# Linear attention and a squared-ReLU FFN on one core: attention chunks 4 to 9 in pairs on quarters of the array, chunks 10 to 23 by halves, the block-diagonal form dropped

## The chip, the core and the metric

The kernel runs on one core of one Trainium2 chip. The metric is the device time in microseconds of one execution; the median of the runs is compared.

## What is computed

The reference, cut to what matters (B = 4, H = 8, S = 768, D = 64, d_model 512, d_ff 2048):

```python
gamma = 1.0 - 2.0 ** (-5.0 - np.arange(H))
for t in range(S):
    state = gamma[None, :, None, None] * state + np.einsum('bhd,bhe->bhde', k[:, :, t], v[:, :, t])
    y[:, :, t] = scale * np.einsum('bhd,bhde->bhe', q[:, :, t], state)
x = y.transpose(0, 2, 1, 3).reshape(B * S, H * D)
h = np.maximum(x @ w_in, 0.0)
out = h * h @ w_out
```

So there is a decaying linear attention over 768 tokens in each of 4 sequences, and then a two-layer FFN on all 3072 tokens.

## The kernel before

The 3072 tokens are 24 chunks of 128 (6 to a sequence). Within a chunk the attention is done by matmuls: q and k are scaled by powers of gamma and cast to bf16, transposed, multiplied into scores, masked, and multiplied with v; a running state in PSUM (`c_ps`, copied to `s_bd`) carries what earlier chunks add. The FFN works on blocks of chunks, `BLOCKS = [4, 2, 2, ...]`: the first product fills `psf` tiles, ACT applies ReLU into `h`, DVE squares it in place, and the second product gives 128 output rows of 512, which ACT copies to `osb` and SP stores.

The schedule is written out by hand. Instructions go to each engine's queue in program order. The front (the calls after `keep_awake(8, ...)`) does chunks 0 to 3 and the first units of block 0, with `keep_awake` matmuls on an identity matrix in between. After that, the FFN is a stream of numbered pieces (`ffn_pieces`): block 0 has pieces 5 to 16 (first product) and 17 to 32 (second), block 1 has 33 to 40 and 41 to 48, block 2 has 49 to 56 and 57 to 64, and so on, 16 to a block. `put(n, step, ...)` hangs a step of the attention, a load or a cast behind piece n; `before(n)` issues these steps, and then the squares of that piece (`take_squares`), so a step on DVE stands in its queue behind the squares of the pieces before.

Three forms of attention are used:

- in pairs on quarters of the array (chunks 0 to 3, `PAIRED = 4`): two chunks at a time, matmuls of 64 rows by 64 columns in four positions of the array (`scores_pair`, `state_pair`, `outputs_pair`), and `finish_pair` with plain matmuls for what comes from the state;
- block-diagonal (chunks 4 to 11, `attend`): one chunk at a time, the two heads of a pair side by side with zeros off the diagonal (`k_bd`, `v_bd`, `s_bd`), in plain matmuls of 128 columns (`scores` L421, `state` L447, `outputs` L476 and L484). Chunks 4 to 7 are transposed on TensorE (L367, L380), chunks 8 to 11 by DMA and a copy on DVE (`spread_k`);
- by halves (chunks 12 to 23, `attend2`): half chunks of 64 tokens, plain matmuls with 64 columns (`scores2` L682, `state2` L709, `outputs2` L731 and L738), always with DMA transposes.

Blocks 1 and 2 run their first product one chunk at a time (`first_unit`, 128 columns); later blocks take both chunks at once (256 columns). `cast_w` and `cast_w_out` turn the fp32 weights into bf16 on POOL, DVE and ACT. `pack_constants` makes the constants of the half form.

Of the kernel before, what the change touches and what calls it, by code (L numbers as in the profile page):

```python
# [9 lines left out]
FP32 = mybir.dt.float32  # L10
# [9 lines left out]
LDBUFS = 4  # L20


PAIRED = 4

# [3 lines left out]
PACK_FROM = 12  # L28

GROUP = 3  # L30
# [3 lines left out]
def kernel(  # L34
# [32 lines left out]
    ldpool = ctx.enter_context(tc.tile_pool(name="ldpool", bufs=LDBUFS // 2))  # L67
    grpool = ctx.enter_context(tc.tile_pool(name="grpool", bufs=2))
    qspool = ctx.enter_context(tc.tile_pool(name="qspool", bufs=2))
    kspool = ctx.enter_context(tc.tile_pool(name="kspool", bufs=4))  # L70
# [34 lines left out]
    kv_tiles = {}  # L105

    def load_kv(m):
        b, i = chunks[m]
        for name, src, to in (("kn", k, raw_k), ("vn", v, raw_v)):
            if m % 2 == 0:  # L110
                kv_tiles[name] = ldpool.tile([P, 2 * H * D], FP32, name=name)
            t = kv_tiles[name].rearrange("s (c h d) -> s c h d", c=2, h=H)[:, m % 2]
            nc.sync.dma_start(t, src[b, :, i * C : (i + 1) * C, :].rearrange("h s d -> s h d"))
            to[m] = t

    def load(m):
        if m % 2 == 0:
            load_q(m)
        load_kv(m)

    def group_loads(m):

        b, i = chunks[m]
        for name, src, to in (("kg", k, raw_k), ("vg", v, raw_v)):
            t = grpool.tile([P, 2 * GROUP, NPAIR, D], FP32, name=name)
            for h in range(H):
                p, hh = divmod(h, 2)
                rows = slice(64 * hh, 64 * (hh + 1))
                nc.sync.dma_start(
                    t[rows, :, p, :],  # L130
                    src[b, h, i * C : (i + GROUP) * C, :].rearrange("(w s) d -> s w d", s=64),
                )
                yield
            for j in range(GROUP):
                to[m + j] = t[:, 2 * j : 2 * j + 2].rearrange("s u p d -> s (u p) d")
# [36 lines left out]
    def exponents(pattern, step, name, logs, parts=(slice(0, P),)):  # L172
# [15 lines left out]
    ex_k = exponents([[C, NCH], [0, H]], 1, "ex_k", lng)  # L188
    qf = const.tile([P, NCH, H], FP32)
    nc.scalar.activation(qf[:], ex_q[:], AF.Exp)  # L190
    kf = const.tile([P, NCH, H], FP32)
    kfp = const.tile([P, NCH, H], FP32)
    nc.scalar.activation(kfp[:], ex_q[:], AF.Exp, scale=-1.0)
    nc.scalar.activation(kf[:], ex_k[:], AF.Exp, scale=-1.0)
# [14 lines left out]
    cmask = const.tile([P, 2, C // 2], BF16)  # L209
    nc.gpsimd.memset(cmask[:], 0.0)  # L210
    nc.gpsimd.affine_select(
        out=cmask[:],
        in_=cmask[:],
        compare_op=ALU.is_gt,
        fill=1.0,
        base=0,
        pattern=[[-1, 2], [-2, C // 2]],
        channel_multiplier=1,
    )
# [39 lines left out]
    v_bds = [const.tile([P, NPAIR, 4, D], BF16, name=f"v_bd{j}") for j in range(4)]  # L259
    k_bds = [const.tile([P, NPAIR, 2, C], BF16, name=f"k_bd{j}") for j in range(2)]  # L260
    s_bds = [const.tile([P, NPAIR, 2, D], BF16, name=f"s_bd{j}") for j in range(3)]
    ks_bd2s = [const.tile([P, 2 * NPAIR, 2, D], BF16, name=f"ks_bdp{j}") for j in range(2)]

    v_bd2s = [t.rearrange("s p (c hh) d -> s (p c) hh d", hh=2) for t in v_bds[2:]]
    def zero_on_scalar(out, rows=slice(0, P)):
        shape = list(out.shape)
        nc.scalar.activation(
            out, ident[rows, None, 0 : shape[2]].to_broadcast(shape), AF.Copy, scale=0.0
        )

    for t in k_bds:
        nc.vector.memset(t[0:64, :, 1, :], 0.0)
        nc.vector.memset(t[64:128, :, 0, :], 0.0)
    for j, t in enumerate(v_bds[:2]):
        zero_on_scalar(t[:, :, 1:3, :].rearrange("s p hh d -> s p (hh d)"))
        if j < 2:
            zero_on_scalar(s_bds[j][0:64, :, 1, :], slice(0, 64))
            zero_on_scalar(s_bds[j][64:128, :, 0, :], slice(64, 128))
# [49 lines left out]
    def zero_off_diagonal(t, hh):  # L328
        nc.vector.memset(t[halves[hh], :, 1 - hh, :], 0.0)

# [11 lines left out]
    def scale_kv(m):  # L342
        b, i = chunks[m]
        ks = kspool.tile([P, H, D], BF16, name="ks")
        nc.vector.tensor_tensor(
            out=ks[:],
            in0=raw_k.pop(m)[:],
            in1=kf[:, i, :, None].to_broadcast([P, H, D]),
            op=ALU.mult,
        )  # L350
        v_bd = v_bds[m % 2]
        vn = raw_v.pop(m)
        nc.gpsimd.tensor_copy(  # L353
            v_bd[:, :, ::3, :], vn.rearrange("s (p hh) d -> s p hh d", hh=2)
        )
        at[m].update(ks=ks, v_bd=v_bd)

# [3 lines left out]

    def transpose_q(m, split=False):
        qs = at[m].pop("qs")
        tp = ps_tp.tile([P, 2, NPAIR, C], BF16, name="tp")
        for r in range(2):
            for p in range(NPAIR):
                nc.tensor.transpose(tp[:, r, p, :], qs[:, r, 2 * p : 2 * p + 2, :], ident[:])  # L367
        qT = qTpool.tile([P, 2, NPAIR, C], BF16, name="qT")
        if split:
            nc.scalar.activation(qT[:, 0], tp[:, 0], AF.Copy)  # L370
            nc.vector.tensor_copy(qT[:, 1], tp[:, 1])
        else:
            nc.scalar.activation(qT[:], tp[:], AF.Copy)
        give_qT(m, qT)

    def transpose_k(m, pool=ps_tp, name="tp", split=False):
        a = at[m]
        tp = pool.tile([P, 2, NPAIR, C], BF16, name=name)
        for p in range(NPAIR):
            nc.tensor.transpose(tp[:, 0, p, :], a["ks"][:, 2 * p : 2 * p + 2, :], ident[:])  # L380
        k_bd = k_bds[m % 2]
        for hh in range(2):
            rows = slice(64 * hh, 64 * (hh + 1))
            if split and hh == 1:
                nc.vector.tensor_copy(k_bd[rows, :, hh, :], tp[rows, 0, :, :])
            else:
                nc.scalar.activation(k_bd[rows, :, hh, :], tp[rows, 0, :, :], AF.Copy)
        a["k_bd"] = k_bd
# [9 lines left out]
    def dma_transpose_k(m):  # L398
        a = at[m]
        kT = kTpool.tile([P, 2 * NPAIR, C], BF16, name="kT")  # L400
        nc.sync.dma_start_transpose(kT[:, 0:NPAIR], a["ks"].rearrange("s h d -> s (h d)"))
        a["kT"] = kT

    def spread_k(m):
        a = at[m]
        kT = a.pop("kT")
        k_bd = k_bds[m % 2]
        for hh in range(2):
            rows = slice(64 * hh, 64 * (hh + 1))
            nc.vector.tensor_copy(k_bd[rows, :, hh, :], kT[rows, 0:NPAIR])  # L410
        a["k_bd"] = k_bd

    def scores(m, half, pool=ps_st, name="st"):
        a = at[m]
        if half == 0:
            a["pt"] = ptpool.tile([P, NPAIR, 2, C], BF16, name="pt")
        st = pool.tile([P, 2, 2, C], FP32, name=name)
        for pp in range(2):
            p = 2 * half + pp
            for hh in range(2):  # L420
                nc.tensor.matmul(  # L421
                    st[:, pp, hh, :],
                    lhsT=a["k_bd"][:, p, hh, :],
                    rhs=a["qT"][:, :, p, :],
# [623 lines left out]
```

## Time and profile before

| what | value |
|---|---|
| median of 3 runs | 215.16 us (215.15 to 215.17) |
| profiled execution | 214.9 us, of which the span from first to last instruction is 213.1 us |
| TensorE busy | 205.4 us (96%) |
| VectorE (DVE), ScalarE (ACT), GpSimd (POOL) busy | 130.2, 116.1 and 49.7 us |
| first FFN matmul | 19.0 us |
| last FFN matmul starts | 209.9 us |
| moved by DMA | 39.65 MB |

Times inside the profiled execution are counted from its first instruction. Busy time of TensorE adds up overlapped matmuls of a pipelined engine, so the mean duration of a matmul in a row is its latency, not the time that it holds the engine.

### The profile page before, as it was taken

To read this page: it belongs to the slowest core of one execution; us is meant where nothing else is said; L and a number is where in the kernel's file an instruction comes from. 1 tells how busy PE (TensorE), PEld (TensorE's weight loads), DVE (VectorE), ACT (ScalarE), POOL (GpSimd) and SP (SyncE) were. 2 spreads that over 40 slices of the span, in tenths; PEclk is the share of its full clock that TensorE was granted. 3 is DMA by queue.
4 is the path that set the end of the run, shared out by engine and by line. 5 is a ranking of instruction groups with operands and counts; after the bars stand their busy time and mean duration, and the time that the engine had idled before them with its cause. 6 is when DMAs were issued, how large, how long until landed. Compare 5 with 4: busy or idle time off the path is not lost.

```text
span 213.1 us, 5212 instructions
## 1 busy us (share of the span) xinstructions
PE 205.4 (96%) x2119; PEld 142.1 (67%) x2119; DVE 130.2 (61%) x257; ACT 116.1 (54%) x216; POOL 49.7 (23%) x106
## 2 busy tenths in 40 slices
PE   6888999999999999999999999999999999999994
PEld 1466644558966975875875875875965965965853
DVE  4796885165585696695495595593694693640410
ACT  8374885258853653652663663652753754643631
POOL 5332456321110411008122223033121223000000
PEclk9999999999999999999999999999999999999999
DMA  6999999999989796579999598799597432601102
GB/s 167 290 321 381 387 385 244 298 242 258 267 212 200 189 196 145 159 179 174 176 203 198 134 219 182 180 235 174 132 191 174 102 76 73 102 0 52 49 0 98
DMA packets 90551, 39.65 MB, mean 186 GB/s; under 512 B 66336, under 2 KB 84000, under 8 KB 90528
## 3 DMA queue, kind: packets, MB, share of 16 engines
q1 hardware_dynamic: 90528, 39.33, 78.8%
q8 instruction: 16, 0.26, 0.6%
q14 instruction: 7, 0.06, 0.1%
HBM read 27.26 MB, written 6.29 MB: 157 GB/s over the span
## 4 chain that ended last, share of the span: by engine, by line
PE 87%; DMA 5%; DVE 2%; POOL 2%; ACT 1%; issue 1%; SPq 1%; POOLq 0%; ACTq 0%
PE psf L778 38%; PE psf L836 37%; DMA qn<-in_q_dram 3%; DMA vn<-in_v_dram 2%; PE st L421 1%; PE y L484 1%; PE y L738 1%; PE st L682 1%; PE c_ps L709 1%; PE y L731 1%; POOL qs L507 1%; DVE pt L568 1%; DVE pt L428 1%; PE y L476 1%; PE c_ps L586 1%
## 5 line engine op out<-in xcount | busy, mean ns | idle before, releaser
L778 PE MATMUL psf<-xt,w_in_bf 128*128 128x256 bf16 (+2 forms) x880 | 90.6, 259 | 0.2 <-ACT xt L492 0.2
L836 PE MATMUL psf<-w_out_bf,h 128*128 128x512 bf16 (+2 forms) x400 | 89.6, 371 | 0.0
L778 PEld LDWEIGHTS <-w_in_bf 128*128 128x128 bf16 x880 | 71.4, 98 | 11.6 <-issue 0.3
L787 ACT ACTIVATE h<-psf 128x512 bf16<-128x512 f32 x96 | 56.9, 596 | 22.1 <-PE psf L778 19.4
L836 PEld LDWEIGHTS <-h 128*128 128x128 bf16 x400 | 36.3, 98 | 35.1
L758 DVE TENSOR_TENSOR h<-h 128x512 bf16<-128x512 bf16 x96 | 43.7, 472 | 20.6 <-ACT h L787 19.6
L846 ACT ACTIVATE osb<-psf 128x512 f32<-128x512 f32 (+2 forms) x25 | 14.5, 580 | 28.6 <-PE psf L836 28.5
L719 DVE CAST s_bd<-c_ps 64x256 bf16<-64x256 f32 x22 | 9.4, 428 | 27.0 <-ACT s_bd L718 26.8
L657 POOL CAST v<-vg 128x512 bf16<-128x512 f32 x12 | 7.7, 644 | 54.4 <-PE c_ps L709 19.5
L660 POOL CAST v_bd<-vg 64x512 bf16<-64x512 f32 x24 | 15.9, 664 | 17.6 <-PE y L738 16.9
L428 DVE TENSOR_TENSOR pt<-st,cmask 128x512 bf16<-128x512 f32 x16 | 11.1, 691 | 14.3 <-PE st L421 14.0
L644 DVE TENSOR_TENSOR ks_bdp<-kg,kf 64x512 bf16<-64x512 f32 x24 | 18.3, 763 | 0.4
L353 POOL CAST v_bd<-vn 128x512 bf16<-128x512 f32 x8 | 5.7, 718 | 36.5 <-PE y L484 22.6
L745 ACT ACTIVATE xt<-y 128x512 bf16<-128x512 f32 x12 | 8.9, 741 | 9.6 <-PE y L738 9.6
L334 DVE TENSOR_TENSOR qs<-qn,qf 128x1024 bf16<-128x1024 f32 x10 | 12.1, 1213 | 1.8 <-DMA qn<-in_q_dram 1.8
L718 ACT ACTIVATE s_bd<-c_ps 64x256 bf16<-64x256 f32 x22 | 8.1, 366 | 8.8 <-PE c_ps L709 8.8
L492 ACT ACTIVATE xt<-y 128x512 bf16<-128x512 f32 x8 | 6.0, 749 | 5.5 <-PE y L484 5.2
L301 POOL CAST w_out_bf<-w_stage 128x512 bf16<-128x512 f32 x12 | 7.5, 667 | 5.5 <-DMA w_stage<-in_moe_w_out_dram 5.5
L689 DVE TENSOR_TENSOR pt<-st,cmask 128x512 bf16<-128x512 f32 x12 | 8.3, 691 | 0.4
L313 PE MATMUL y<-ident 128*128 128x512 bf16 (+1 forms) x18 | 6.4, 470 | 2.1 <-POOL ident L199 2.1
L709 PEld LDWEIGHTS <-ks_bdp 128*128 128x128 bf16 x88 | 5.6, 98 | 2.6
L738 PE MATMUL y<-pt,v_bd 128*128 128x64 bf16 x96 | 7.0, 193 | 0.0
(100 smaller groups left out, 169.0 us busy)
## 6 DMA issues: line engine op xcount, KB each, us to landing
qn<-in_q_dram SPq DMA_DIRECT2D x12, 512.0 KB, 5.7
out_dram<-osb SPq DMA_DIRECT2D x23, 256.0 KB, 2.5
w_stage<-in_moe_w_out_dram SPq DMA_DIRECT2D x4, 1024.0 KB, 12.3
w_stage<-in_moe_w_in_dram SPq DMA_DIRECT2D x3, 1024.0 KB, 11.7
kg<-in_k_dram SPq DMA_DIRECT2D x32, 96.0 KB, 3.8
vg<-in_v_dram SPq DMA_DIRECT2D x32, 96.0 KB, 3.3
kn<-in_k_dram SPq DMA_DIRECT2D x8, 256.0 KB, 5.5
vn<-in_v_dram SPq DMA_DIRECT2D x8, 256.0 KB, 5.9
```

The lines of the kernel that those rows point to most:

```text
L334: nc.vector.tensor_tensor(out=qs[:], in0=raw_q.pop(m).rearrange("s h r d -> s r h d"), in1=qf[:, i : i + 2, :, None].to_broadcast([P, 2, H ...
L428: nc.vector.tensor_tensor(out=a["pt"][:, 2 * half : 2 * half + 2], in0=st[:], in1=cmask.rearrange("s r t -> s (r t)")[:, None, None, :].to ...
L644: nc.vector.tensor_tensor(out=ks[rows, :, hh, :], in0=kn[rows], in1=kf2[rows, i].rearrange("s u p -> s (u p)")[:, :, None].to_broadcast([6 ...
L660: nc.gpsimd.tensor_copy(v_bd[rows, :, hh, :], vn[rows])
L719: nc.vector.tensor_copy(s_bd[halves[1], :, 1, :], c[halves[1]])
L738: nc.tensor.matmul(yv, lhsT=a["v_bd"][:, u * NPAIR + p], rhs=a["pt"][:, u * NPAIR + p, :].rearrange("s (r t) -> s r t", r=2), start=not inter,
L745: nc.scalar.activation(xts[tb][:, :, off : off + C].rearrange("e p (s r) -> e p r s", r=2), y[:], AF.Copy,)
L758: nc.vector.tensor_mul(hv, hv, hv)
L778: nc.tensor.matmul(hp, lhsT=w_in_bf[g][:, cb, fq * 128 : (fq + 1) * 128], rhs=xts[tb][:, cb, cols], start=(cb == 0), stop=(cb == NCB - 1),)
L787: nc.scalar.activation(hv, hp[:], AF.Relu)
L836: nc.tensor.matmul(op[:], lhsT=h_of(tb, f)[:, 0, j * C : (j + 1) * C], rhs=w_out_bf[g][:, fq, cols], start=(f == 0), stop=(f == NFB - 1),)
L846: nc.scalar.activation(osb[:, cols], op[:], AF.Copy)
```

## The change

`PAIRED`, `GROUP` and `LDBUFS` go; `FRONT = 4`, `PACK_FROM = 10` and `GROUPS = [2, 3, 3, 3, 3]` come. The functions of the block-diagonal form (`scale_kv`, `transpose_q`, `transpose_k`, `dma_transpose_k`, `spread_k`, `scores`, `state`, `outputs`, `attend`, `load_kv`) and their constants (`kf`, `cmask`, `v_bds`, `k_bds`) are removed. Chunks 4 to 9 take the pair form, through a new `attend_pair` and `transpose_both`; chunks 10 and 11 take the half form. The pair form gets tiles of its own (`ks_pairs`, `v_pairs`), which before it shared with the half form, so the zeros of `ks_bd2s` and of the third `s_bd` are set in the front. In the front, `state_pair` uses 8 matmuls with 128 columns on 64 rows instead of 16 quarter matmuls; there are fewer `keep_awake` matmuls, and the first half units of the FFN stand ahead of `outputs_pair(2, ...)`. Blocks 1 and 2 run their first product like the later blocks. `pack_constants` moves from place 50 to 36, and the loads move.

```diff
-PAIRED = 4
+FRONT = 4
 DMA_FROM = 8
-PACK_FROM = 12
-GROUP = 3
+PACK_FROM = 10
+GROUPS = [2, 3, 3, 3, 3]
...
+    def transpose_both(m, what):
+        a = at[m]
+        if what == "q":
+            to = qTpool.tile([P, 2, NPAIR, C], BF16, name="qT")
+        else:
+            to = kTpool.tile([P, 2 * NPAIR, C], BF16, name="kT")
+            to = to.rearrange("e (r p) s -> e r p s", r=2)
+        a[what + "T"] = to
+        fr = a[what + "s"]
+        if m >= DMA_FROM:
+            nc.sync.dma_start_transpose(
+                to.rearrange("e r p s -> e (r p) s"), fr.rearrange("s r h d -> s (r h d)")
+            )
+            return
+        tp = ps_tp.tile([P, 2, NPAIR, C], BF16, name="tp")
+        for r in range(2):
+            for p in range(NPAIR):
+                nc.tensor.transpose(tp[:, r, p, :], fr[:, r, 2 * p : 2 * p + 2, :], ident[:])
+        nc.scalar.activation(to[:, 0], tp[:, 0], AF.Copy)
+        nc.vector.tensor_copy(to[:, 1], tp[:, 1])
...
     def state_pair(m, j):
+        if i + j == NCH - 1:
+            return
...
+        wide = b == 0
         for p in range(NPAIR):
             for r in range(2):
+                begin = i + j == 0 and p == 0 and r == 0
+                if m < FRONT:
+                    nc.tensor.matmul(
+                        c[:, p],
+                        lhsT=a["ks"][halves[j], r, 2 * p : 2 * p + 2, :],
+                        rhs=a["v"][halves[j], r, 2 * p : 2 * p + 2, :],
+                        start=begin,
...
+                    continue
                 for hh, head in enumerate(halves):
                     nc.tensor.matmul(
-                        c[head, p, hh, :],
+                        c[head, p, hh if wide else 0, :],
...
         for hh, head in enumerate(halves):
-            nc.scalar.activation(s_bd[head, :, hh, :], c[head, :, hh, :], AF.Copy)
+            to, fr = s_bd[head, :, hh, :], c[head, :, hh if wide else 0, :]
+            if hh == 0 or m < FRONT:
+                nc.scalar.activation(to, fr, AF.Copy)
+            else:
+                nc.vector.tensor_copy(to, fr)
...
-        elif tb <= 2:
-
-            for c in range(nch):
-                for g in range(NQ):
-                    first_unit(tb, g, c)
-                    yield
...
-    keep_awake(8, pool=ps_y, name="y")
+    keep_awake(6, pool=ps_y, name="y")
...
-    keep_awake(2, C)
+    keep_awake(1, C)
     transpose_pair(0, "k", 1, *f, on_scalar=False)
-    keep_awake(1, C)
...
     transpose_pair(2, "q", 0, *f, on_scalar=False)
-    keep_awake(1, C)
+    keep_awake(1)
     transpose_pair(2, "q", 1, *f, on_scalar=False)
-    keep_awake(2)
+    keep_awake(1)
     end_awake()
...
     transpose_pair(2, "k", 0, *f, on_scalar=False)
-    keep_awake(2, C)
     transpose_pair(2, "k", 1, *f, on_scalar=False)
...
-    keep_awake(1)
     state_pair(2, 0)
     cast_w("in", 0, (1,), "GGVV")
-    outputs_pair(2, 0, ((ps_y, "y"), f))
-    keep_awake(2)
-    end_awake()
+    first_unit(0, 0, 0, (0,))
+    first_unit(0, 0, 1, (0,))
+    outputs_pair(2, 0, ((ps_y, "y"), st))
     outputs_pair(2, 1)
     finish_pair(2, 0)
     finish_pair(2, 1, on_scalar=False)
-    first_unit(0, 0, 0, (0,))
-    first_unit(0, 0, 1, (0,))
+    first_unit(0, 0, 0, (1,))
+    first_unit(0, 0, 1, (1,))
     state_pair(2, 1)
     cast_w("in", 1, on="VVGG")
-    first_unit(0, 0, 0, (1,))
-    first_unit(0, 0, 1, (1,))
...
-    load(4)
+    load_q(4)
+    load_pair(4, "kn", k, raw_k)
...
+    def attend_pair(m, q, qT, k, kT, v, scores, d):
+        for r in range(2):
+            put(q + r, scale_pair_q, m, r)
+            put(k, scale_pair_k, m, r)
+            put(scores + 2 * r, scores_pair, m, r, (st, tp))
+            put(d - 1, outputs_pair, m, r, ((ps_y, "y"), tp))
+        put(qT, transpose_both, m, "q")
+        put(kT, transpose_both, m, "k")
+        put(v, cast_pair_v, m)
+        put(scores + 2, state_pair, m, 0)
+        put(d, finish_pair, m, 0)
+        put(d, finish_pair, m, 1, False)
+        put(d, state_pair, m, 1)
...
-    for m, place in ((5, 10), (6, 14), (7, 18)):
-        put(place, load, m)
+    put(9, load_pair, 4, "vn", v, raw_v)
+    put(11, load_q, 6)
+    put(12, load_pair, 6, "kn", k, raw_k)
+    put(13, load_pair, 6, "vn", v, raw_v)
...
-    put(26, cast_w_out, 3, "GGGS")
-    attend(4, 21, (23, 25, 27, 29, 31))
-    attend(5, None, (28, 30, 32, 33, 35))
-    attend(6, 30, (33, 35, 37, 39, 42))
-    attend(7, None, (40, 42, 44, 46, 49))
-    put(50, pack_constants)
-    for j, t in enumerate([s_bds[2]] + ks_bd2s + v_bd2s):
+    put(25, cast_w_out, 3, "GGGS")
+    attend_pair(4, 21, 23, 24, 25, 28, 26, 31)
+    put(24, load_q, 8)
+    put(26, load_pair, 8, "kn", k, raw_k)
+    put(30, load_pair, 8, "vn", v, raw_v)
+    put(36, pack_constants)
+    for j, t in enumerate(v_bd2s):
         for hh in range(2):
-            put(51 + 3 * j + hh, zero_off_diagonal, t, hh)
+            put(37 + 3 * j + hh, zero_off_diagonal, t, hh)
+    attend_pair(6, 36, 38, 39, 40, 40, 42, 47)
+    attend_pair(8, 46, 48, 48, 50, 51, 57, 63)
...
-    for m, place in zip(range(PACK_FROM, NCHUNK, GROUP), (43, 67, 92, 116)):
-        loads = group_loads(m)
+    for size, place in zip(GROUPS, (31, 46, 70, 94, 118)):
+        loads = group_loads(m, size)
         for j in range(2 * H):
-            put(place + 3 * j // 2, next, loads)
+            put(place + 5 * j // 4, next, loads)
...
```

## The prediction

> **What bounds the kernel now.** I read the page's engine totals first, then the table by stage, the matmul groups with shapes kept apart, and the chain of waits in order of time.
>
> ```profile
> PE 205.4 (96%) x2119; PEld 142.1 (67%) x2119; DVE 130.2 (61%) x257; ACT 116.1 (54%) x216; POOL 49.7 (23%) x106
> ```
> ```profile
> 0.00:10.00 10.00, 7.49 (x63) 3.44 (x64) 5.98 (x16) 6.22 (x13) 4.31 (x23) 1.00 0.90 225
> 10.00:20.00 10.00, 8.23 (x198) 5.58 (x195) 8.34 (x17) 6.08 (x13) 3.58 (x7) 1.00 1.12 343
> 20.00:30.00 10.00, 10.00 (x99) 6.17 (x98) 7.46 (x22) 8.00 (x17) 4.30 (x10) 1.00 1.05 386
> 70.00:80.00 10.00, 9.73 (x143) 8.24 (x141) 8.16 (x22) 5.59 (x11) 2.88 (x15) 1.00 0.93 184
> ```
> The columns are stretch, length, then busy PE, weight load, DVE, ACT, POOL, then clock, DMA share and GB/s. From 20 us on TensorE is full except for two dents (the 40-60 and 70-80 stretches); before 20 us it waits on loads and on a chain of small steps, with DMA saturated. So the time is: the moment the FFN stream starts, plus the TensorE work behind it, plus its stalls.
>
> ```profile
> L836 PE MATMUL psf<-w_out_bf,h 128*128 128x512 bf16 x368 | 86.1, 379 | 0.0
> L778 PE MATMUL psf<-xt,w_in_bf 128*128 128x256 bf16 x512 | 60.4, 273 | 0.0
> L778 PE MATMUL psf<-xt,w_in_bf 128*128 128x128 bf16 x320 | 19.8, 219 | 0.2 <-ACT xt L492 0.2
> L682 PE MATMUL st<-qT,kT 128*128 128x64 bf16 x96 | 4.8, 193 | 0.0
> L421 PE MATMUL st<-qT,k_bd 128*128 128x128 bf16 x64 | 6.3, 219 | 0.3 <-DVE pt L428 0.3
> ```
> Durations there are pipeline latencies. What counts is start to start in an unbroken run, which I took from the timeline: 216 ns for 512 columns, 109.2 for 256, 55.8 for 128, 29.1 for 64.
>
> ```profile
> 19.20 0.89 PE psf L778 x16
> 20.09 0.37 PE c_ps L586 x16
> 20.46 13.15 PE psf L778 x96
> ...
> 49.38 0.64 ACT xt L492
> 50.06 1.05 PE psf L778 x16
> ...
> 70.78 0.27 POOL ex_k_i L175
> 71.40 0.23 DVE ex_k_f L177
> 71.66 0.21 DVE ex_k_f L178
> 71.90 0.70 DVE pt L428
> 72.64 0.38 PE st L421 x4
> ```
> The chain shows the insert of 16 quarter matmuls at 20.1 us and the two dents: 50.06 (block 1 waits 0.35 us for xt behind an osb copy on ACT) and 72.64 (a mask on DVE waits for pack_constants, which waits on POOL; start to start 491 ns instead of 56, so 0.43 us).
>
> **The change, part by part** (TensorE time unless said).
>
> *1. Block form dropped.* Its 212 matmuls of 128 columns for chunks 4 to 11 (64 L421, 24 L447, 64 L484, 28 L476, 16 L380, 16 L367) leave: 212 x 0.0558 = 11.83 us.
>
> *2. Chunks 10 and 11 by halves.* 60 matmuls of 64 columns (state 8+4, scores 16, outputs 32): 60 x 0.0291 = 1.75.
>
> *3. Chunks 4 to 9 on quarters.* 32 transposes and 20 finish matmuls of 128 columns: 52 x 0.0558 = 2.90. The rest runs in 64*64 form, already seen in the front. First to last start: 16 scores 0.20 (9.07 to 9.27), 16 state matmuls 0.25 (20.02 to 20.27), 32 output matmuls 0.45 (11.83 to 12.28). Getting in costs 0.093 (149 ns start to start at 20.02 instead of 56), getting out 0.125 to 0.148 (20.27 to 20.39; 9.27 to 9.42), plus 0.01 on the next step. So an insert is 0.45 for scores alone, 0.75 for scores with state behind, 0.70 for outputs, 0.47 for state alone; of these there are 3, 3, 3 and 2 (chunk 5 ends its sequence and has no state): 1.36 + 2.24 + 2.11 + 0.95 = 6.66. Quarters in all: 9.56. Sum of 1 to 3: -11.83 + 1.75 + 9.56 = **-0.52**. Nearly all of it is from the halves; chunks 4 to 9 come out 0.18 dearer, because state on quarters (0.47) replaces 4 plain matmuls (0.22). The Trainium skill, "TensorEngine Tiling (Array Packing)", Key Properties, says that a change of tiling mode drains TensorE, and its Theoretical Speedup table offers up to 2x for each small dimension. The rows agree with the drain (0.22 to 0.24 a visit); by the table alone, 4x and no drains, the 6.66 us would be an estimated (192 x 0.0558 + 80 x 0.0291) / 4 = 3.3 and the total 3.4 us better.
>
> *4. Blocks 1 and 2 of the first product* go from 256 matmuls at 0.0558 (14.28) to 128 at 0.1092 (13.98): **-0.31**.
>
> *5. Front.* The last masks of chunk 2 now end near 17.75 instead of 17.42: state_pair in the front becomes 8 matmuls of 128 columns (0.45 instead of 0.25, twice, with a drain before the quarters), which delays the chunk 2 k transposes from 13.57 to about 13.9. But 16 FFN matmuls (0.89 us) move ahead of outputs_pair(2,0), into time now spent on idle matmuls, and need only the half of w_in 0 cast by 16.2. The other half lands at 18.27 and POOL casts it until 18.78 and 19.23; DMA order up to there is unchanged, so the second 16 run 18.8 to 20.1, state (0.62) to 20.7, two units of 0.89 to 22.5. Now the first 512-column piece starts at 23.08: **-0.55**. Bound below: its weights (w_in 1, first half) are cast at 21.94, so -1.1; above, if the unexplained 0.81 us "issue" gap at 17.47 to 18.28 moves behind 19.2: +0.3. The removed constants (cmask, kf, v_bd and k_bd zeros) sat on POOL, DVE and ACT before 5.2 us, under the wait for q, so nothing.
>
> *6. Old dents.* pack_constants moves to place 36, where POOL has no load to wait on: **-0.43**. Block 1 waits for xt as before; xt(4) now stands behind the third osb copy: about 0.2 instead of 0.35: **-0.16**.
>
> *7. New waits.* Place n is after FFN piece n. Chunk 6: q is scaled at places 36 and 37, transposed at 38; k scaled at 39, transposed at 40, on pieces of 0.873. DVE runs in order, and a square ends about 1.25 after its piece, so place 36's work starts 0.38 late: constants 0.50 (71.40 to 71.90), q half 0.62, square 0.36, zero memset 0.2, q half 0.68: ends at 2.74 after piece 36. Transposes of half two could start at 1.97 and wait 0.8. Queued behind them on PE are pieces 39 and on; on DVE then square 0.36, memset 0.2, qT copy 0.4, square 0.36, k halves 1.3, ending at 5.26, while PE reaches that half of k at 4.95: 0.35. Together **+1.13**. Ends: 0 if DVE starts each row on time, 1.5 with one more square ahead. Chunk 4 has no squares around it: q and k are ready within 0.05 of need. Its v load now stands behind w_out 3 on SP's queue: w_out 3 lands at 41.35, the next 512 KB by 43.74 (POOL's casts start there), two casts of 0.6 end near 44.9, and state_pair(4,0) at place 28 comes at 45.0, with scores of r = 1 ahead and piece 29 queued behind: **+0.05**, up to 0.5. At place 64, state2(10) waits for the c_ps copy on DVE: **+0.09**. Chunk 8's k goes by DMA transpose at place 50 for place 57 (6 us against 2.5 to 4.2 landing): nothing; if SP were held 2 us by the group loads of chunks 10 to 14 that now start there (0.6 us an issue), still nothing. Those loads come 6 pieces or more ahead of their casts. Loads of chunks 4 to 9 move to 512-byte rows (32 ns a packet against 21 for 256): earlier landings, hidden.
>
> Sum: -0.52 - 0.31 - 0.55 - 0.43 - 0.16 + 1.13 + 0.05 + 0.09 = **-0.70**. The profiled execution took 214.9 (span 213.1 and 1.8 around it): 214.2. The median of the runs is 0.26 above it: 215.16 - 0.7 = about 214.4. A comparison of this kernel can tell about 0.2% (0.43 us) from no change.
>
> **Rivals.**
> (A) the sum above: 214.4, own range 213.9 to 214.9; chance 0.45.
> (B) The DVE waits of part 7 are covered (relus and squares run earlier than I place them): -1.83, 213.3. For: DVE is only 61% busy. Against: it is in order, and at 72.64 the same constants did hold PE. Chance 0.23.
> (C) Slower: instruction supply. The gap at 17.47 to 18.28 lies between two quarter matmuls with no semaphore, after a burst of short instructions; a 16 KB instruction packet moved at 15.84 to 16.97. If visits in 64*64 form, 64 to 96 instructions in half a microsecond, meet such a gap in the body, each costs 0.8; from two of the 11 visits on the result is slower: +0.9, 216.1; three give 216.9. Against: 48 matmuls at 11.55 to 12.28 ran without one, and the 171 matmuls of 50-60 us too. Chance 0.17.
> (D) The clock. Matmuls of 512 columns start 427 ns apart until 5.05, 128-column ones 107 apart at 7.63 and 56 from 7.95. With 6 idle matmuls instead of 8 and fewer behind them, the array may stay at the slow rate: until about 11.4 it adds 0.3 to the scores, hidden before 18.8; until 14.8 it doubles the chunk 0 state, output and chunk 2 transpose work, some 0.9 past that bound: 215.3, no change. The Trainium skill, "TensorE: Matmul & The Clock Gate", Part 1, has a free-running 3.4 us window of activity that sets the rate; the trace agrees with the two rates. Chance 0.07.
> (E) Several waits of part 7 at their upper ends cancel the gain: 215.1. Chance 0.08.
>
> **How the numbers follow.** Faster by over 0.2%: most of A (0.36 of 0.45) and B: 0.59. Within: the rest of A, D and E, less what of those is over: 0.21. Slower: C and the tails of D and E: 0.20. The range reaches from B with the front's lower bound partly in (213.0) to C with two gaps (216.1).
>
> **What would show it.** First 512-column piece at 22.5 (front); no matmul of block form; 11 visits in 64*64 form with 0.09 in and 0.13 out; 16-matmul runs of 256 columns in blocks 1 and 2; PE waiting on DVE qs and ks in the tp transposes near 54 to 59 us (A) or not (B); gaps inside quarter matmuls with no releaser (C); 107 ns starts after 8 us (D). Wrong altogether if the steady part behind chunk 12 changes, or PE waits for a load in chunks 4 to 9.

## The result: 217.7 us, slower by 1.4%

The four runs of the changed kernel took 217.19 to 220.06 us, median 217.7, against 215.16 before: a ratio of 1.0143 (95% interval 1.0109 to 1.0177). The forecast was 214.4. The profiled run took 217.19 us, its span (from the first to the last instruction) 215.4 where the old one was 213.1, so 2.3 us are to be found between the two traces. It was the fastest of the four; what the run of 220.06 lost is not shown.

**Engine totals of the changed kernel.** TensorE is busy 0.4 us less than before in a span that is 2.3 us longer: work did not grow, waiting did.

```profile
span 215.4 us, 5207 instructions
PE 205.0 (95%) x2121; PEld 136.6 (63%) x2121; DVE 132.3 (61%) x253; ACT 110.3 (51%) x208; POOL 52.9 (25%) x107
```

**The table by stage of the changed kernel** (stretch, length, busy TensorE, weight load, DVE, ACT, POOL, then clock, DMA share, GB/s). Before, TensorE was busy 9.87 us of 40-50, 9.94 of 50-60 and 9.73 of 70-80; now 9.66, 8.68 and 8.52. First two lines of the old kernel, then three of the changed one:

```profile
40.00:50.00 10.00, 9.87 (x74) 5.49 (x72) 3.72 (x6) 6.61 (x12) 2.97 (x5) 1.00 1.26 254
50.00:60.00 10.00, 9.94 (x171) 9.67 (x171) 6.23 (x13) 7.86 (x15) 0.77 (x1) 1.00 1.04 262
```
```profile
40.00:50.00 10.00, 9.66 (x127) 4.85 (x126) 5.14 (x10) 3.41 (x7) 5.94 (x20) 1.00 1.11 293
50.00:60.00 10.00, 8.68 (x78) 6.76 (x76) 6.74 (x16) 6.40 (x12) 1.21 (x2) 1.00 0.74 217
70.00:80.00 10.00, 8.52 (x86) 6.89 (x84) 8.32 (x15) 5.37 (x9) 2.50 (x3) 1.00 0.67 147
```

**The waits of TensorE in the changed kernel** (us in total, times, longest) name three places: L389 are the transposes of chunks 4 and 6, L403 the scores, here of chunk 8.

```profile
PE st L403 <- DMA kT<-ks_pair: 1.5, 1, 1.5
PE tp L389 <- DVE qs L329: 1.0, 2, 0.8
PE tp L389 <- DVE ks_pair L339: 0.7, 3, 0.3
```

This view counts idle time behind modelled ends of matmuls, so short waits, as that of chunk 4's scores at 43.14, hardly show in it. Start to start, less the usual distance of two such matmuls, the same waits cost 0.89 us at chunk 4 (41.00, 41.60 and 43.14 us), 2.17 at chunk 6 (56.29, 57.44, 59.92 and 60.52) and 1.64 at chunk 8 (79.68). All costs of waits below are taken this way.

**The chain of waits at chunk 6** (start, length, what ended last there):

```profile
54.54 0.53 DVE ex_k_f L157
...
55.09 0.54 DVE ex_k_f L158
55.63 0.60 DVE qs L329
56.23 0.33 DVE h L627
56.57 0.27 DVE v_bd L232
56.84 0.56 DVE qs L329
...
57.44 0.41 PE tp L389 x4
...
57.88 0.61 ACT qT L390
...
58.51 0.42 DVE qT L391
58.93 0.33 DVE h L627
59.26 1.21 DVE ks_pair L339 x2
```

For five microseconds DVE is the end of everything: a cast and a product of `pack_constants`, half of q, a square, a memset, the other half of q. Then DVE's copy of the second half of the transposed q starts 0.03 us after ACT's copy of the first half ends, and k's scaling is queued behind it. The cast and the product of the constants last 0.60 and 0.54 us here, beside POOL's cast of v (54.36 to 55.57); in the old kernel they took 0.22 and 0.21.

**SP's queue in the changed kernel, 71 to 77 us** (start, length, DMA issue). k of chunk 8 is scaled by 72.19, but its transpose is issued at 76.31, behind a transpose of 2.04 us and four group loads; it lands at 79.64, and TensorE came for it at 78.04.

```profile
71.51 2.04 SPq L382 DMA_TRANSPOSE qT<-qs  x1
73.60 0.61 SPq L109 DMA_DIRECT2D vg<-in_v_dram  x1
74.26 0.61 SPq L109 DMA_DIRECT2D kg<-in_k_dram  x1
74.92 0.62 SPq L109 DMA_DIRECT2D vg<-in_v_dram  x1
75.59 0.61 SPq L109 DMA_DIRECT2D kg<-in_k_dram  x1
76.31 1.27 SPq L382 DMA_TRANSPOSE kT<-ks_pair  x1
```

### The profile page after: what moved, and what is told of

Its sections match the earlier page's. It is cut to its first block, busy times and chain, and to the rows that moved or that the text cites. A ratio compares the mean times of both kernels' runs of the same rounds, so it can differ in the third digit from the quotient of the medians.

```text
span 215.4 us, 5207 instructions
## 1 busy us (share of the span) xinstructions
PE 205.0 (95%) x2121; PEld 136.6 (63%) x2121; DVE 132.3 (61%) x253; ACT 110.3 (51%) x208; POOL 52.9 (25%) x107
## 4 chain that ended last, share of the span: by engine, by line
PE 87%; DVE 5%; DMA 4%; ACT 2%; issue 1%; SPq 0%; ACTq 0%; DVEq 0%
PE psf L699 38%; PE psf L647 36%; DMA kn<-in_k_dram 3%; DMA kT<-ks_pair 2%; PE st L546 2%; PE y L607 2%; DVE ks_pair L339 1%; PE y L600 1%; PE c_ps L573 1%; PE st L403 1%; DVE pt L411 1%; PE y L470 1%; PE tp L389 1%; PE c_ps L436 1%; PE y L277 1%
## 5 line engine op out<-in xcount | busy, mean ns | idle before, releaser
L647 PE MATMUL psf<-xt,w_in_bf 128*128 128x256 bf16 (+2 forms) x752 | 89.2, 275 | 0.0
L647 PEld LDWEIGHTS <-w_in_bf 128*128 128x128 bf16 x752 | 68.8, 98 | 13.1 <-DVE xt L500 0.5
L656 ACT ACTIVATE h<-psf 128x512 bf16<-128x512 f32 x96 | 57.1, 597 | 22.2 <-PE psf L647 19.8
L521 POOL CAST v<-vg 128x512 bf16<-128x512 f32 x14 | 10.5, 748 | 72.5 <-DMA vg<-in_v_dram 38.7
L508 DVE TENSOR_TENSOR ks_bd<-kg,kf 64x512 bf16<-64x512 f32 x28 | 21.0, 749 | 0.5
L614 ACT ACTIVATE xt<-y 128x512 bf16<-128x512 f32 x14 | 10.4, 743 | 11.2 <-PE y L607 11.2
L582 ACT ACTIVATE s_bd<-c_ps 64x256 bf16<-64x256 f32 x25 | 9.2, 366 | 8.8 <-PE c_ps L573 8.8
L458 ACT ACTIVATE s_bd<-c_ps 64x256 bf16<-64x256 f32 x13 | 4.9, 376 | 10.2 <-PE c_ps L446 8.9
L553 DVE TENSOR_TENSOR pt<-st,cmask 128x512 bf16<-128x512 f32 x14 | 9.7, 691 | 0.4
L295 DVE TENSOR_TENSOR qs<-qn,qf 128x1024 bf16<-128x1024 f32 x7 | 8.5, 1217 | 0.0
L411 DVE TENSOR_TENSOR pt<-st,maskp 128x512 bf16<-128x512 f32 x8 | 5.5, 692 | 4.6 <-PE tp L403 4.1
L573 PEld LDWEIGHTS <-ks_bd 128*128 128x128 bf16 x100 | 6.3, 98 | 3.1 <-DVE s_bd L460 0.5
L600 PE MATMUL y<-qT,s_bd 128*128 128x64 bf16 x104 | 7.9, 193 | 0.0
L600 PEld LDWEIGHTS <-s_bd 128*128 128x128 bf16 x104 | 7.1, 98 | 0.9
```

The costliest lines, as they stand in the source:

```text
L508: nc.vector.tensor_tensor(out=ks[rows, :, hh, :], in0=kn[rows], in1=kf2[rows, i].rearrange("s u p -> s (u p)")[:, :, None].to_broadcast([6 ...
L521: nc.gpsimd.tensor_copy(v2[:], vn[:])
L600: nc.tensor.matmul(yv, lhsT=last_state(m, u)[:, p], rhs=half_of(a["qT"], p, u), start=True, stop=False,)
L614: nc.scalar.activation(xts[tb][:, :, off : off + C].rearrange("e p (s r) -> e p r s", r=2), y[:], AF.Copy,)
L647: nc.tensor.matmul(hp, lhsT=w_in_bf[g][:, cb, fq * 128 : (fq + 1) * 128], rhs=xts[tb][:, cb, cols], start=(cb == 0), stop=(cb == NCB - 1),)
L656: nc.scalar.activation(hv, hp[:], AF.Relu)
```

## Experiments: the three waits, each alone and together

Theory W: the loss is three schedules that are too tight. Rival F: the pair form on quarters is itself dearer than priced, and the waits only take the place of others. Each of three kernels gives one pair of chunks more time; a fourth does all three. Each ratio is to runs of the old kernel taken beside (medians 214.88 to 215.14). The arguments of `attend_pair` are the chunk and the places of q, the q transpose, k, the k transpose, v, the scores and the outputs.

```diff
-    attend_pair(4, 21, 23, 24, 25, 28, 26, 31)
+    attend_pair(4, 20, 22, 22, 24, 28, 26, 31)   # k4
-    put(36, pack_constants)
+    put(30, pack_constants)                      # k6
-            put(37 + 3 * j + hh, zero_off_diagonal, t, hh)
+            put(43 + 2 * j, zero_off_diagonal, t, hh)
-    attend_pair(6, 36, 38, 39, 40, 40, 42, 47)
+    attend_pair(6, 29, 38, 32, 40, 40, 42, 47)
-    attend_pair(8, 46, 48, 48, 50, 51, 57, 63)
+    attend_pair(8, 46, 48, 48, 48, 51, 57, 63)   # k8
```

**Chunk 8 alone (k8).**

> The changed kernel with one number changed: the DMA transpose of chunk 8's k is issued at place 48 instead of 50, so on SP's queue it stands ahead of four group loads. Theory W (the loss is waits of TensorE at three places, chunks 4, 6 and 8): the wait of 1.5 us of the chunk 8 scores on the transposed k (79.7 us in the profile) falls under 0.3, and the span goes from 215.4 to about 213.9. Rival F (the quarter form itself costs, its visits and drains, and the waits only hide a delay that would come out elsewhere): the span stays within 0.4 of 215.4.

Measured: 216.73 us, ratio to the old kernel 1.0076 (1.0045 to 1.0106). The wait at chunk 8 is gone, but 0.76 us come back at 90.35, where the scores of chunks 10 and 11 wait for a DMA transpose.

**Chunk 6 alone (k6).**

> The changed kernel with DVE's work for chunk 6 taken out of the first product of block 1: q scaled at places 29 and 30 and k at 32, pack_constants at 30, the zeros of v_bd at 43 and 45; transposes stay at 38 and 40. Theory W: the waits of TensorE on DVE qs and ks at 56.3, 57.4, 59.9 and 60.5 us (0.39 + 0.92 + 0.50 + 0.37 = 2.2 us) go, except some 0.2 for the copies out of the transposes; span about 213.4. Rival F: within 0.4 of 215.4. Rival P (the wait moves on): chunk 8's wait grows by as much as chunk 6's falls, since its q and k stand on DVE behind the same pieces; span 214.5 to 215.4.

Measured: 215.88 us, 1.0041 (1.0011 to 1.0071). All four waits of chunk 6 are gone, that of chunk 8 (1.55) stays and does not grow, so rival P falls.

**Chunk 4 alone (k4).**

> The changed kernel with chunk 4 one place or two earlier: q scaled at 20 and 21, its transposes at 22, k scaled at 22 ahead of the copy of q, transposes of k at 24. Theory W: the waits at 41.0, 41.6 and 43.1 us (0.18 + 0.37 + 0.34 = 0.9 us) go if k has landed by about 37.5 us, as q had by 36.2; span about 214.5. If k lands later than 38.5, half of it stays. Rival F: within 0.4 of 215.4.

Measured: 216.69 us, 1.0052 (1.0021 to 1.0083). The waits at 41.0, 41.6 and 43.1 are gone; chunks 6 and 8 wait 2.17 and 1.71, about as before.

In order of k8, k6 and k4, the medians fall by 1.0, 1.8 and 1.0 us, where theory W has 1.5, 2.0 and 0.9. The spans that it forecast (213.9, 213.4 and 214.5) were missed: the traces have 216.1, 214.0 and 215.5. Their first 512-column pieces (there the full stream of the FFN begins) start at 23.53, 22.74 and 23.04 us instead of 22.24, and chunk 4's waits, 0.89 in the changed kernel's trace, are 1.41 in `k8` and 1.30 in `k6`. With these terms, beside the waits named above, the three spans come out to about 0.1 us.

**All three (all3).**

> The changed kernel with all three edits (chunk 4, chunk 6, chunk 8). Theory W: the waits add up, 0.9 + 2.0 + 1.4, and the span comes to about 211 us, 2 below the kernel before (213.1). Rival F: above 213.1, since the form costs. Rival P: between 212 and 214 with a new wait on DVE or SP in block 2.

Measured: 214.07 us (212.63 to 214.62), 0.994 (0.9916 to 0.9964). Its table by stage:

```profile
40.00:50.00 10.00, 9.63 (x129) 5.19 (x131) 6.12 (x12) 4.39 (x9) 5.60 (x20) 1.00 1.16 297
50.00:60.00 10.00, 9.95 (x104) 7.98 (x103) 5.41 (x13) 6.13 (x11) 1.31 (x2) 1.00 0.75 217
70.00:80.00 10.00, 9.79 (x108) 6.48 (x108) 7.76 (x15) 4.44 (x8) 3.55 (x6) 1.00 0.80 175
```

TensorE has its 50-60 and 70-80 stretches back, with every quarter visit in place. The span is 210.9, so 4.5 us below the changed kernel and 2.2 below the old one. Theory W holds and F falls: the form was not dear, its supply was late. In time, though, the median gains 3.6 us where the profile, which was the fastest of the ten runs, gains 4.5, and the runs spread over 2 us. The next runs look for that.

## Experiments: what spreads the runs

In the profiles so far the first 512-column piece started anywhere from 22.2 to 23.5 us, and TensorE's full rate came for good between 10.3 and 13.1 us instead of 7.9. (The old kernel's runs beside these lie at 214.87 to 215.17, but for four of 31 at 216.6 to 216.9, which no trace explains.) Theory K puts the spread on the fewer idle matmuls, rival L on the loads.

**Idle matmuls back in the changed kernel (awake).** The same edit makes `all3_awake` from `all3`, and its reverse, in the old kernel, `before_less`:

```diff
-    keep_awake(6, pool=ps_y, name="y")
+    keep_awake(8, pool=ps_y, name="y")
...
-    keep_awake(1, C)
+    keep_awake(2, C)
     transpose_pair(0, "k", 1, *f, on_scalar=False)
+    keep_awake(1, C)
...
-    keep_awake(1)
+    keep_awake(1, C)
     transpose_pair(2, "q", 1, *f, on_scalar=False)
-    keep_awake(1)
+    keep_awake(2)
```

> The changed kernel with the idle matmuls of the front put back to the old numbers (8 at the start instead of 6, 2 and 1 of 128 columns around the chunk 0 k transposes, 1 of 128 columns and 2 of 512 around the chunk 2 q transposes), the rest as in the changed kernel, its waits at chunks 4, 6 and 8 too. Theory K (with fewer idle matmuls the array is granted its full rate at a moment that differs from run to run, 10.3 to 13.1 us in the profiles so far against 7.9 in the old kernel, and the first 512-column piece moves with it): 128-column matmuls 56 ns apart from about 8 us, first 512-column piece at 22.2, and the runs lie within 0.5 us of a median near 217.0. Rival L (the spread comes from the loads, whose queue is the same): spread of 2 us as before, median 217.6.

> The same idle matmuls put back into the version that has the three waits taken away (214.07 at the median, 212.63 to 214.62). Theory K: median near 212.6, runs within 0.5 us of it, so 1.2% below the old kernel. Rival L: 214.1 again, with the same spread.

> The old kernel with nothing changed but the idle matmuls of its front, at the numbers of the changed kernel (6 at the start instead of 8, one of 128 columns instead of three around the chunk 0 k transposes, 1 and 1 of 512 columns around the chunk 2 q transposes). Theory K: the full rate comes at 10 to 13 us, the runs spread over 1 to 2 us and the median is 0.3 to 1.3 above 214.9 (216.0 taken). Rival L: 214.9, within 0.2.

Measured: `awake` 218.03 us (217.85 to 218.62), 1.0128 (1.0097 to 1.016); `all3_awake` 213.8 (212.87 to 214.43), 0.9929 (0.9907 to 0.9952); `before_less` 215.85 (215.32 to 216.21) against 215.14, 1.0026 (1.0007 to 1.0046).

In the old kernel theory K is right but for the spread, which was 0.9 us where 1 to 2 were forecast. The timeline shows four 128-column transposes, first of the old kernel, then of `before_less`; the group takes 0.40 us at the full rate and 0.61 at the slow one:

```profile
8.15 0.40 PE L544 MATMUL psf<-ident,ks_bdp 128*128 128x128 bf16 x4
```
```profile
8.19 0.61 PE L544 MATMUL psf<-ident,ks_bdp 128*128 128x128 bf16 x4
```

Its first 512-column piece moves from 23.08 to 24.28 us, and the median by 0.7. In the changed kernel K is wrong: with the full rate there by 7.7 us, the first piece starts at 22.70, later than the 22.24 of the changed kernel, and the medians stay 1.0 and 1.2 us above its forecasts (217.0 and 212.6). Only the spread of `awake` is smaller, 0.8 us. POOL's casts of `w_in` 0 show why, in the changed kernel and in `awake`:

```profile
15.51 0.75 POOL L255 CAST w_in_bf<-w_stage 128x256 bf16<-128x256 f32 x2 [0.34 <-DMA w_stage<-in_moe_w_in_dram]
17.03 0.75 POOL L255 CAST w_in_bf<-w_stage 128x256 bf16<-128x256 f32 x2 [0.78 <-DMA w_stage<-in_moe_w_in_dram]
```
```profile
15.52 0.75 POOL L255 CAST w_in_bf<-w_stage 128x256 bf16<-128x256 f32 x2 [0.33 <-DMA w_stage<-in_moe_w_in_dram]
18.43 0.93 POOL L255 CAST w_in_bf<-w_stage 128x256 bf16<-128x256 f32 x2 [2.16 <-DMA w_stage<-in_moe_w_in_dram]
```

The second half of `w_in` 0 is 1.4 us later. Its 16 completion updates (one from each DMA engine) and the 16 KB instruction packet that moves at that time, in the traces:

| kernel | full rate from | packet from | 15th and 16th update | first 512-column piece |
|---|---|---|---|---|
| before | 7.93 | 15.84 | 16.90, 18.25 | 23.08 |
| awake | by 7.7 | 16.09 | 16.93, 18.37 | 22.70 |
| all3_awake | 6.73 | 16.04 | 16.96, 18.36 | 22.69 |
| sp50 (below) | 10.79 | 16.34 | 16.88, 18.59 | 22.91 |
| changed | 10.54 | 16.20 | 16.87, 16.98 | 22.24 |
| all3 | 10.26 | 16.21 | 16.86, 16.91 | 22.23 |
| k4 | 12.19 | 16.95 | 16.91, 16.96 | 23.04 |
| k8 | 13.14 | 17.38 | 17.00, 17.06 | 23.53 |
| before_less | 12.68 | 17.15 | 16.90, 16.95 | 24.28 |
| k6 | 4.89 to 8.31, then 11.72 | 16.79 | 16.88, 16.89 | 22.74 |
| awake_pack30 (below) | 11.19 | 16.55 | 16.82, 16.85 | 22.76 |
| all3_state (below) | 5.52 | 16.10 | 16.98, 18.34 | 22.66 |
| all3_k2 (below) | 6.25 | 16.01 | 16.98, 18.30 | 22.62 |
| best (below) | by 6.0 | 16.05 | 16.95, 18.30 | 22.63 |

Fifteen updates come by 17.0 in every trace. The last comes with them, or 1.3 to 1.7 us later. In the late ones its 4-byte packet ends 0.01 (`sp50`) to 0.8 us (before) after the end of the instruction packet of 1.1 us, in the latter with a few rows of `w_in` in between, which points to one DMA engine with the instruction packet in front; the records do not name the engine. The time of the packet alone does not decide (16.34 was early enough in `sp50`, 16.20 too late in the changed kernel), but by and large it comes early where TensorE runs early. So in these profiles an array that wakes early pays with a late half of `w_in` (piece at 22.6 to 22.9), one that wakes late pays in its own matmuls (22.7 to 23.5), and the profiled runs of the changed kernel and of `all3`, at 22.24 and 22.23, had neither. Nor do the idle matmuls alone set the moment: `awake_pack30` has the same ones as `awake`, and its full rate came at 11.19. The Trainium skill, "DMA: Bandwidth & Descriptors", section "Why a DMA increments its semaphore by 16 and not by 1", says that each engine posts its own completion and only all sixteen mean that the data is there; the 15 and 1 of the table agree.

A late front is paid for a second time at chunk 4. DVE's scaling of k there takes 1.28 us in the changed kernel's trace (from 40.26) and 1.70 in `awake` (from 40.72), where more of it lies beside POOL's casts of `w_out` 3 (from 40.96 and 41.11). Chunk 4's waits are 0.89 us in the one and 1.30 in the other, and 1.30 too in `k6`, `awake_pack30` and `sp50`, which have the same places for chunk 4.

**State moved, to move the packet (all3_state).**

```diff
-    state_pair(2, 0)
     cast_w("in", 0, (1,), "GGVV")
     first_unit(0, 0, 0, (0,))
     first_unit(0, 0, 1, (0,))
+    state_pair(2, 0)
```

> The version with the three waits taken away and the idle matmuls put back, with state_pair(2, 0) moved behind the two first FFN units. In ten profiles TensorE's 16 KB instruction packet of the front came at 15.84 to 16.09 us in three and at 16.2 to 17.4 in seven; in the three, the last packets of the second half of w_in 0 ended at 17.6 to 17.8 (casts from 18.3), in the seven at 16.3 to 16.5 (casts possible from 17.0). Theory I (the packet is moved when TensorE's stream reaches a fixed instruction, and holds up the rows of w_in that share its DMA engine): with eight matmuls fewer ahead, the same instruction comes behind the wait for the first half of w_in, the packet after 16.2, casts from 17.0, and the first 512-column piece at 22.2 to 22.4 instead of 22.69. Rival R (the early packet and the late rows only go together by chance of the run): casts from 18.3 again, first piece at 22.7 or later.

Measured: 213.45 us, 0.993 (0.9917 to 0.9943). The packet came at 16.10 again, updates at 16.98 and 18.34, the first piece at 22.66. Eight matmuls fewer ahead of it did not move the packet, so theory I's forecast failed. A fixed place in TensorE's instructions is not refuted by it, though: in the twelve profiles of the changed kernel and its variants the packet starts between 0.26 us before and 0.08 us after the first FFN matmul (L647), which itself starts anywhere from 16.01 to 17.63. In this run that matmul started at 16.03, against 16.08 in `all3_awake`, so the edit did not make it later. What sets the packet off stays open; that an early packet and a late last update go together holds here too.

**k transposes of chunks 10 and 11 a place earlier (all3_k2).** The chain of waits of `all3_awake` has, near 81 and 89 us, these two pieces, each the flight of such a transpose and each ahead of the scores that waited for it:

```profile
81.31 4.21 DMA kT<-ks_bd
...
89.25 4.83 DMA kT<-ks_bd
```
```diff
-        put(d - 13, transpose_k2, m)
+        put(d - (14 if m < 12 else 13), transpose_k2, m)
```

> The version with the three waits taken away and the idle matmuls put back, with the DMA transposes of k for chunks 10 and 11 one place earlier. There TensorE waited 0.28 and 0.64 us for them (0.16 and 0.13 without the idle matmuls put back). If SP's queue is what is late: both waits go, the time falls by 0.3 to 0.9 and the runs lie closer together. If the scaled k itself is late: no change.

Measured: 213.24 us (212.57 to 214.07), 0.9919 (0.9902 to 0.9937). Both waits are gone, and the two stretches are full:

```profile
70.00:80.00 10.00, 10.00 (x112) 6.67 (x110) 8.13 (x15) 4.56 (x8) 3.67 (x6) 1.00 0.77 173
80.00:90.00 10.00, 10.00 (x136) 7.39 (x134) 6.00 (x12) 5.08 (x10) 0.00 (x0) 1.00 0.95 187
```

Against `all3_awake` the span falls by 1.0 us (212.0 to 211.0) and the time by about 0.5, though the intervals of the two ratios overlap. These waits were 0.13 to 0.77 us in the four profiles of this family that had them, so they can be a part of the spread; that they are is not shown, since the runs of `all3_k2` spread over 1.5 us, as those of `all3_awake` (1.6).

**All of these (best).**

> All of these together: the three waits taken away, the idle matmuls back, state_pair(2, 0) behind the first units, k transposes of chunks 10 and 11 one place earlier. By the sum of the theories: first 512-column piece at 22.3, no wait over 0.2 us from 40 us on, span 210.7 to 211.3, time 212.5 to 213.1 at the median against 214.9 to 215.2 before. If the front's time and the late transposes do not go back to these causes, 213.8 as without the two moves.

Measured: 213.43 us (212.84 to 213.62), 0.9921 (0.9909 to 0.9933). The first piece is at 22.63 (updates 16.95 and 18.30), and one wait of 0.49 is left at 93.73, for a DMA transpose. The forecast (first piece at 22.3, no wait over 0.2, 212.5 to 213.1) was missed: the front is as in `all3_state`, and the earlier place does not always take the wait away. It isn't better than `all3_k2`; both beat both kernels.

## Experiments: inside the waits of chunks 6 and 8

**Constants earlier (awake_pack30).** The kernel `awake` with `pack_constants` at place 30, and nothing else.

> As the kernel with the idle matmuls put back, and pack_constants at place 30 instead of 36; chunk 6's own steps stay where they are. It splits the 2.17 us that TensorE waits at chunk 6. If the constants ahead of the q scaling on DVE are the cause (0.60 and 0.54 us of casts): the waits before the q transposes (1.3 in all) shrink to 0.2, those before the k transposes stay at 0.3 to 0.9, time 1.1 to 1.7 below the kernel with the idle matmuls alone. If it is the tight places of chunk 6 themselves: the q waits stay above 0.8 and the time falls by less than 0.5.

Measured: 217.81 us, 1.011 (1.0075 to 1.0145), so 0.2 below `awake`, which the intervals do not tell from nothing; chunk 8's wait is 1.79 here and 1.55 in `awake`. Of chunk 6's waits only the first (0.39) is gone; the next is 0.915 as before. DVE and POOL in its timeline:

```profile
55.05 0.76 DVE L627 TENSOR_TENSOR h<-h 128x512 bf16<-128x512 bf16 x1 [0.45 <-ACT h L656]
55.74 1.09 DVE L329 TENSOR_TENSOR qs<-qn,qf 128x512 bf16<-128x512 f32 x1
56.75 0.41 DVE L627 TENSOR_TENSOR h<-h 128x512 bf16<-128x512 bf16 x1
57.16 0.27 DVE L232 MEMSET v_bd<- 64x256 uint32 x1
57.36 0.62 DVE L329 TENSOR_TENSOR qs<-qn,qf 128x512 bf16<-128x512 f32 x1
```
```profile
54.92 1.36 POOL L352 CAST v_pair<-vn 128x512 bf16<-128x512 f32 x2 [5.99 <-DMA vn<-in_v_dram]
```

The second half of q stands behind two squares, the first half and a memset in DVE's queue, and the first square cannot start before ACT's ReLU; with the transpose only one place behind, that is too late even when the constants are out of the way. So taking the constants away gives 0.39 of the 2.17. The rest is not the places alone: the first square and the first half of q, beside POOL's cast, took 0.76 and 1.09 us, where alone they take 0.41 and 0.62 to 0.68, an estimated 0.8 us together, nearly as much as the wait of 0.915 behind them. No run separates the two; `k6`, which moved q and k themselves, took all four waits away.

**Group loads behind chunk 8's transpose (sp50).** The changed kernel with the second group of loads at place 50.

```diff
-    for size, place in zip(GROUPS, (31, 46, 70, 94, 118)):
+    for size, place in zip(GROUPS, (31, 50, 70, 94, 118)):
...
-        put(place + 22, next, loads, None)
+        put(place + 20, next, loads, None)
```

> The changed kernel with the loads of the group of chunks 12 to 14 started at place 50 instead of 46, behind chunk 8's k transpose in its place; the transpose itself stays at place 50. Theory S (the 1.64 us that TensorE waits for chunk 8's k are SP's queue: the q transpose of 2.04 us and four loads of 0.61 to 0.62 us each stand ahead of the k transpose, which is issued at 76.31 though k is scaled by 72.2): k is issued at about 73.6 and lands near 77.2, before TensorE comes for it at 78.0; the wait is gone and the time 1.3 to 1.7 below the changed kernel, near 216.2. Rival T (place 50 is too late for the transfer itself, whatever SP does): the wait stays above 1 us and the time within 0.5 of 217.7.

Measured: 217.5 us, 1.0119 (1.0104 to 1.0133); the first piece, at 22.91, gives 0.67 away and chunk 4, at 1.30, another 0.41. TensorE no longer waits for the transpose, so SP's queue was what held it. But 0.41 and 0.58 us of new waits stand at 81.72 and 82.31, on DVE: the scores of the other half need the PSUM tile that the masks (L411) read. The chain of `sp50` there:

```profile
78.45 1.00 DVE ks_bd L508
...
79.47 0.28 DVE h L627
...
80.11 0.83 DVE h L627
...
80.97 1.30 DVE pt L411 x2
...
82.31 0.24 PE tp L403 x2
```

DVE's scaling and the squares behind it in the timelines of `sp50`, where POOL casts from 77.88 on, and of `all3`, where POOL starts at 75.65:

```profile
77.75 1.70 DVE L508 TENSOR_TENSOR ks_bd<-kg,kf 64x512 bf16<-64x512 f32 x2
79.47 1.47 DVE L627 TENSOR_TENSOR h<-h 128x512 bf16<-128x512 bf16 x2
```
```profile
73.53 1.40 DVE L508 TENSOR_TENSOR ks_bd<-kg,kf 64x512 bf16<-64x512 f32 x2
74.96 0.76 DVE L627 TENSOR_TENSOR h<-h 128x512 bf16<-128x512 bf16 x2
```

The net of a wait taken away is 1.64 less 0.99: when SP is no longer late, DVE is next.

## Why the prediction was wrong

| step of the prediction | predicted | measured |
|---|---|---|
| 1 to 3, attention on TensorE | -0.52 | visits as priced: 0.093 in, 0.125 to 0.148 out |
| 4, 256 columns in blocks 1 and 2 | -0.31 | 16 matmuls in 1.75 us, as priced |
| 5, front | -0.55 | -0.84 (22.24 instead of 23.08) |
| 6, old dents | -0.43, -0.16 | the first gone; 0.17 left of 0.35 |
| 7, chunk 6 | +1.13 | +2.17 |
| 7, chunk 4 | +0.05 | +0.89 |
| 7, place 64 | +0.09 | +0.13 |
| 7, chunk 8 | 0 | +1.64 |
| sum | -0.70 | +2.55; the span grew by 2.3 |

The matmul side was right, and rival C with its gaps in the supply of instructions fell: no quarter visit of the body waits without a releaser. What failed is part 7, in three terms.

- *Chunk 8: "nothing; if SP were held 2 us by the group loads ... still nothing."* SP got to the transpose 4.1 us after k was scaled, held by the q transpose of 2.04 as well as the loads, and the flight took 3.3: 7.4 us where TensorE's stream gave 5.9. The prediction counted 2 us of loads and left out the transpose ahead of them. This was the largest single error.
- *Chunk 6: +1.13.* The mechanism was named and the size was too small. The constants were taken at 0.50 from the old trace, where POOL was setting a mask (memset and select) at the time; beside POOL's cast of v they take 1.14. And the copy of q^T on DVE, taken to run beside ACT's, starts when ACT's ends, which puts both halves of k 0.6 later. Together they pass the upper end given (1.5). Not all of that was there to be saved: with the constants out of the way (`awake_pack30`) only 0.39 came back, and POOL's cast stretched a square and half of q instead. (The 0.35 for k would be 0.31 by the prediction's own 5.26 and 4.95, which changes nothing.)
- *Chunk 4: +0.05, "ready within 0.05 of need".* Readiness of q and k was checked, the chain behind them was not: DVE copies q^T after ACT (until 40.34), scales both halves of k (until 41.55), and TensorE's four transposes, ACT's copy and DVE's copy then run one after the other until the scores at 43.14. In four traces with a later front it is 1.30.

The front gained more than predicted: the last update of `w_in`'s second half came at 16.98 instead of 18.25. The prediction took the 18.27 of the old trace as a property of the load; the traces point to the instruction packet in its way. In seven of the fourteen profiles the update was late, so the gain is in part the luck of the profiled run.

Rival D (the clock, chance 0.07, worth 0.9 us) is real as a mechanism: in the old kernel alone it costs 0.7 us at the median. In the changed kernel it does not decide the median, since the early array got the late half of `w_in`; rival L, the loads, is nearer there. The Trainium skill, "TensorE: Matmul & The Clock Gate", Part 1, has a free-running window of about 3.4 us, so that the moment depends on where the window stands when work begins; the clock record of `k6`, full from 4.89 to 8.31, slow to 11.72, then full, shows such steps of 3.41 us. Rival E had the right shape, waits at their upper ends, but its ends (0.5 for chunk 4, 1.5 for chunk 6, none for chunk 8) reached only 215.1.

With the three schedules loosened the forecast's sum is found again: the terms without part 7 come to -2.3 with the front as measured, and `all3` has a span 2.2 us below the old kernel's. That is to about 0.4 us, what `all3` still waits at 83.8, 85.0 and 93.0, and for the fastest of its ten runs; its median is 0.8 below that of the old runs beside it.

## What to carry to other kernels

A step that moves to another form is priced by its whole chain on every engine that it visits, with what stands ahead of it in each queue at that moment: here TensorE's cost was right to a few tenths and the three waits cost ten times that. For a DMA issued behind others, count the issues ahead of it on its queue from the moment that its input is ready. And when one wait is taken away, look who is next at the same place: here, at chunk 8, DVE or the next transposes gave back 46 to 60% of it, while chunks 4 and 6 gave back nothing at their own place.

## What the runs showed that was not expected

- A 16 KB instruction packet of 1.1 us seems to hold back the last of 16 completion updates of a load by 1.3 to 1.7 us, and so the whole load, when it comes first (that both share one DMA engine is inferred). The last update was late in all six profiles with the packet at 16.10 or before and in one of the eight with a later one.
- DVE and POOL stretch each other: squares of 0.41 us took 0.72 and 0.83, the constants' cast of 0.22 took 0.60, POOL's cast of 0.61 took 1.02. Beside POOL's memset and mask select of the old kernel the constants' cast and product took 0.22 and 0.21. The Trainium skill, "SBUF — State Buffer", section "Who interferes with whom", has an exclusive lock in which the loser blocks for the whole instruction; the trace of `awake_pack30` agrees to about 0.15 us an instruction. POOL's first cast, from 54.92, keeps its 0.61 and ends at 55.54; the square begun at 55.05 ends 0.27 after it, POOL's next cast 0.47 after that, and the half of q 0.55 after that, where alone they take 0.41, 0.61 and 0.62 to 0.68. The traces do not show where inside an instruction the time goes.
- A DVE copy of one half of a transposed PSUM tile started 0.03 us after ACT's copy of the other half ended, each time (42.63 and 42.66, 58.47 and 58.51). The timeline names ACT's copy as what released it; why DVE waits for it isn't shown.
